# Forgetting attention, then a spectral mix: head pairs become the outer loop, mode weights are contracted by quarters of d, the decay moves into V, and each engine issues in the order of emission

## The chip, the cores and the metric

The kernel runs on one core of a Trainium2 chip. The metric is the device time of one execution in microseconds. Times are given as the median of several runs, with the lowest and highest beside it where they matter. The profile shows one execution; its span is about 2 us shorter than the time of the same run.

The names in the profiles: PE is the engine for matrix products (PEld its loads of the stationary operand), ACT the scalar, DVE the vector and POOL the general engine. POOL and SP also issue loads and stores, each to a queue of its own; the DMA moves the bytes. The row PEclk is the share of PE's full clock that the profile records as granted. A step is one pass of the changed kernel's inner loop: two heads of one batch.

## The reference, cut to what matters

```python
# q, k, v: (8, 8, 576, 64), f: (8, 8, 576); B=8, H=8, S=576, d=64
cum    = cumsum(log(clip(f, 1e-4, 1)))
scores = q @ k.T / 8 + cum[:, :, :, None] - cum[:, :, None, :]     # causal
attn   = softmax(scores);  x = (attn @ v) as (B, S, 512)
# moe_w_r, moe_w_i: (64, 512, 512), moe_w_ch: (512, 512)
X = rfft(x, axis=1)[:, :64]                       # 64 modes
Yr = Xr @ w_r - Xi @ w_i ;  Yi = Xr @ w_i + Xi @ w_r      # per mode
u = x + irfft(Y) ;  out = u + relu(u @ w_ch)
```

The mode weights are 134 MB in fp32 (2 x 64 x 512 x 512 x 4 bytes). They are read once and cast to bf16 on the way. Each is used for 8 batches only, so reading them is the largest single piece of data movement.

## The kernel before

It has three stages. Attention takes one batch after another, and a batch is four head pairs. The mode stage starts when all batches are transformed, because the contraction of a mode runs over all 512 columns of d. The output stage follows.

```python
# attention of one head pair: 64-row operands, one exponential per head and block
for hp in range(2):
    bp = hp * 64
    pscore = psA.tile([128, 512], F32, tag="sc", name="pscore")
    nc.tensor.matmul(pscore[:Mj, 0:n],
        lhsT=KTs[bp : bp + 64, s0 : s0 + Mj],
        rhs=QTs[bp : bp + 64, s0 + c0 : s0 + c0 + n], start=True, stop=True)
    pss.append(pscore)
for hp in range(2):
    nc.scalar.activation(et[:Mj, c0 : c0 + n], pss[hp][:Mj, 0:n], ACT.Exp,
        bias=biasAll[:Mj, jb, bh : bh + 1], scale=scale)      # decay as a bias
# ... (mask, AV, normalisation, transform of a whole batch: cut)

# the mode stage: one mode at a time, all of d
wpool = ctx.enter_context(tc.tile_pool(name="wpool", bufs=6))
for m in range(NM):
    wb = wpool.tile([128, 2, NEB, D], BF16, tag="wb", name="wb")
    nc.gpsimd.dma_start(wb[:, 0, :, :], moe_w_r[m].rearrange("(dc p) e -> p dc e", p=128))
    nc.gpsimd.dma_start(wb[:, 1, :, :], moe_w_i[m].rearrange("(dc p) e -> p dc e", p=128))
    A = psM.tile([128, 2, NEB, 2 * B], F32, tag="A", name="A")
    for t in range(2):
        for ebx in range(NEB):
            for dc in range(NEB):                 # contraction over the four quarters of d
                nc.tensor.matmul(A[:, t, ebx, :],
                    lhsT=wb[:, t, dc, ebx * 128 : (ebx + 1) * 128],
                    rhs=_strided(XT[:, dc, 0, m, 0:1], [[1, 2], [NM * 2, B]]),
                    start=(dc == 0), stop=(dc == NEB - 1))
    # ... (As <- A on ACT, two combining ops on DVE into YT: cut)
    if m % 8 == 3 and (m // 8) < B:
        xw_for_batch(m // 8)                      # XW = x @ w_ch of one batch
# ... (the output stage: cut)
```

The softmax here doesn't subtract the row's maximum and nothing guards it: scores larger than these inputs give would overflow.

Of the kernel before, what the change touches and what calls it, by code (L numbers as in the profile page):

```python
# [21 lines left out]
def kernel(  # L24
# [17 lines left out]
    NSB = 5  # L42
    SBLK = [128, 128, 128, 128, 64]
    NEB = D // 128
    BH = B * H
    scale = 1.0 / math.sqrt(Dh)

    const = ctx.enter_context(tc.tile_pool(name="const", bufs=1))
    xpool = ctx.enter_context(tc.tile_pool(name="xpool", bufs=1))
    wpool = ctx.enter_context(tc.tile_pool(name="wpool", bufs=6))  # L50

    x_all = xpool.tile([128, B, NSB, D], BF16, name="x_all")
    XT = xpool.tile([128, NEB, B, NM, 2], BF16, name="XT")
# [4 lines left out]
    masks.make_identity(nc, ident_bf[:])  # L58
    masks.make_identity(nc, ident_f[:])
    masks.make_upper_triangular(nc, trimask[:], val=1.0, diag=True)  # L60

    iota_p_i = const.tile([128, 1], I32, name="iota_p_i")
    nc.gpsimd.iota(iota_p_i[:], pattern=[[0, 1]], base=0, channel_multiplier=1)
    s_i = const.tile([128, NSB], I32, name="s_i")
    nc.gpsimd.iota(s_i[:], pattern=[[128, NSB]], base=0, channel_multiplier=1)
    s_f = const.tile([128, NSB], F32, name="s_f")
    nc.vector.tensor_copy(s_f[:], s_i[:])
    nc.vector.tensor_scalar(s_f[:], s_f[:], float(S - 1), None, ALU.min)
    ones_row = const.tile([1, 128], F32, name="ones_row")
    nc.vector.memset(ones_row[:], 1.0)  # L70
    negpi = const.tile([128, 1], F32, name="negpi")
    nc.vector.memset(negpi[:], -math.pi)

    bas = const.tile([128, NSB, NM, 2], BF16, name="bas")
    BI = const.tile([128, S], BF16, name="BI")
    cumT = const.tile([128, NSB, BH], F32, name="cumT")
    biasAll = const.tile([128, NSB, BH], F32, name="biasAll")
    wch = const.tile([128, NEB, D], BF16, name="wch")

    TWO_PI_OVER_S = 2.0 * math.pi / S  # L80

    with ExitStack() as sctx:
        ps_setup = sctx.enter_context(
            tc.tile_pool(name="ps_setup", bufs=2, space=bass.MemoryType.PSUM)
        )
        ssb = sctx.enter_context(tc.tile_pool(name="setup_sb", bufs=1))

        gem = ssb.tile([128, NSB], F32, name="gem")
        nc.vector.tensor_scalar(gem[:], s_f[:], 432.0, None, ALU.is_ge)
        spl = ssb.tile([128, NSB], F32, name="spl")  # L90
        nc.vector.tensor_scalar(spl[:], s_f[:], 144.0, None, ALU.add)
        sz = ssb.tile([128, NSB], F32, name="sz")
        nc.vector.scalar_tensor_tensor(
            sz[:], gem[:], -float(S), spl[:], ALU.mult, ALU.add
        )
        S0 = ssb.tile([128, NSB], F32, name="S0")
        C0 = ssb.tile([128, NSB], F32, name="C0")
        nc.scalar.activation(
            S0[:], s_f[:], ACT.Sin, bias=negpi[:, :], scale=TWO_PI_OVER_S
        )  # L100
        nc.scalar.activation(
            C0[:], sz[:], ACT.Sin, bias=negpi[:, :], scale=TWO_PI_OVER_S
        )
        Zt = ssb.tile([128, NSB, NM, 2], F32, name="Zt")
        nc.vector.memset(Zt[:, :, 0, 0], 1.0)
        nc.vector.memset(Zt[:, :, 0, 1], 0.0)
        nc.vector.tensor_scalar(Zt[:, :, 1, 0], C0[:], -1.0, None, ALU.mult)
        nc.vector.tensor_copy(Zt[:, :, 1, 1], S0[:])
        wrot = ssb.tile([128, NSB, 2], F32, name="wrot")
        nc.vector.tensor_copy(wrot[:, :, :], Zt[:, :, 1, :])  # L110
        ta = ssb.tile([128, NSB, 32], F32, name="ta")
        tb = ssb.tile([128, NSB, 32], F32, name="tb")
        M = 2
        while M < NM:
            wr = wrot[:, :, 0]
            wi = wrot[:, :, 1]
            t0 = ssb.tile([128, NSB], F32, name="t0")
            t1 = ssb.tile([128, NSB], F32, name="t1")
            nc.vector.tensor_tensor(t0[:], wr, wr, ALU.mult)
            nc.vector.tensor_tensor(t1[:], wi, wi, ALU.mult)  # L120
            t2 = ssb.tile([128, NSB], F32, name="t2")
            nc.vector.tensor_tensor(t2[:], wr, wi, ALU.mult)
            nc.vector.tensor_tensor(wrot[:, :, 0], t0[:], t1[:], ALU.subtract)
            nc.vector.tensor_scalar(wrot[:, :, 1], t2[:], 2.0, None, ALU.mult)
            Are = Zt[:, :, 0:M, 0]
            Aim = Zt[:, :, 0:M, 1]
            wr_b = _strided(wrot[:, :, 0:1], [[2, NSB], [0, M]])
            wi_b = _strided(wrot[:, :, 1:2], [[2, NSB], [0, M]])
            nc.vector.tensor_tensor(ta[:, :, 0:M], Are, wr_b, ALU.mult)
            nc.vector.tensor_tensor(tb[:, :, 0:M], Aim, wi_b, ALU.mult)  # L130
            nc.vector.tensor_tensor(Zt[:, :, M : 2 * M, 0], ta[:, :, 0:M], tb[:, :, 0:M], ALU.subtract)
            nc.vector.tensor_tensor(ta[:, :, 0:M], Are, wi_b, ALU.mult)
            nc.vector.tensor_tensor(tb[:, :, 0:M], Aim, wr_b, ALU.mult)
            nc.vector.tensor_tensor(Zt[:, :, M : 2 * M, 1], ta[:, :, 0:M], tb[:, :, 0:M], ALU.add)
            M *= 2
        nc.vector.tensor_copy(bas[:, :, :, :], Zt[:, :, :, :])
        coef = ssb.tile([128, 1], F32, name="coef")
        nc.vector.memset(coef[:], 2.0 / S)
        nc.vector.memset(coef[0:2, :], 1.0 / S)
        for sc in range(NSB):  # L140
            ns = SBLK[sc]
            bip = ps_setup.tile([128, 128], F32, tag="sps", name="bip")
            nc.tensor.transpose(
                bip[:, :ns],
                Zt[:ns, sc, :, :].rearrange("p m ri -> p (m ri)"),
                ident_f[:ns, :ns],
            )
            nc.vector.tensor_scalar(  # L148
                BI[:, sc * 128 : sc * 128 + ns], bip[:, :ns], coef[:], None, ALU.mult
            )  # L150

        ft = ssb.tile([BH, S], F32, name="ft")
        nc.sync.dma_start(ft[:], f.rearrange("b h s -> (b h) s"))
        lf = ssb.tile([BH, S], F32, name="lf")
        nc.scalar.activation(lf[:], ft[:], ACT.Ln)
        onesS = ssb.tile([BH, S], F32, name="onesS")
        nc.vector.memset(onesS[:], 1.0)
        cum = ssb.tile([BH, S], F32, name="cum")
        nc.vector.tensor_tensor_scan(
            cum[:], onesS[:], lf[:], 0.0, ALU.mult, ALU.add  # L160
        )
        cum_ps = ps_setup.tile([128, NSB, BH], F32, tag="sps2", name="cum_ps")
        for sc in range(NSB):
            ns = SBLK[sc]
            nc.tensor.transpose(
                cum_ps[:ns, sc, :],
                cum[:, sc * 128 : sc * 128 + ns],
                ident_f[:BH, :BH],
            )
        nc.vector.tensor_copy(cumT[:, 0:4, :], cum_ps[:, 0:4, :])  # L170
        nc.vector.tensor_copy(cumT[:64, 4, :], cum_ps[:64, 4, :])
        nc.vector.memset(cumT[64:128, 4, :], 0.0)
        R_ps = ps_setup.tile([128, BH], F32, tag="sps2", name="R_ps")
        nc.tensor.matmul(
            R_ps[:],
            lhsT=ones_row[0:1, :],
            rhs=cumT[0:1, 2, :],
            start=True,
            stop=True,
        )  # L180
        Rb = ssb.tile([128, BH], F32, name="Rb")
        nc.vector.tensor_copy(Rb[:], R_ps[:])
        nc.vector.tensor_tensor(
            biasAll[:, :, :],
            _strided(Rb[:, :], [[0, NSB], [1, BH]]),
            cumT[:, :, :],
            ALU.subtract,
        )

        wch_f = ssb.tile([128, NEB, D], F32, name="wch_f")  # L190
        nc.sync.dma_start(
            wch_f[:], moe_w_ch.rearrange("(eb p) e -> p eb e", p=128)
        )
        nc.vector.tensor_copy(wch[:], wch_f[:])

    with ExitStack() as actx:
        qkbf = actx.enter_context(tc.tile_pool(name="qkbf", bufs=2))
        vapool = actx.enter_context(tc.tile_pool(name="vapool", bufs=2))
        qtkt = actx.enter_context(tc.tile_pool(name="qtkt", bufs=2))
        epool = actx.enter_context(tc.tile_pool(name="epool", bufs=14))  # L200
        psA = actx.enter_context(
            tc.tile_pool(name="psA", bufs=4, space=bass.MemoryType.PSUM)
        )
        psB = actx.enter_context(
            tc.tile_pool(name="psB", bufs=2, space=bass.MemoryType.PSUM)
        )
# [366 lines left out]
```

## Time and profile before

| | before |
|---|---|
| time, median of 4 runs | 671.9 us (670.98 to 673.73) |
| attention | up to about 308 us |
| mode stage | about 308 to 613 us |
| output stage | to 671.5 us |
| weight loads | 128 of 512 KB (as bf16) |

The page of the kernel before divides the span into 40 slices of 16.8 us. A digit is the busy share in tenths; the GB/s are bytes written into the core's memory, so fp32 weights that are cast count half.

```profile
PE   0169999999999999999888895222222222225996
PEclk9999999999995555555799877555555555555998
DMA  9999391919191914003999999999999999994375
GB/s 199 185 148 150 36 120 9 98 9 99 8 100 11 97 10 26 1 1 58 202 207 206 207 206 206 206 206 206 206 206 206 206 206 207 206 206 81 134 247 184
```

The two rows PE and DMA are complements: attention fills the PE and leaves the DMA mostly idle; the mode stage fills the DMA at 206 GB/s and leaves the PE at two tenths. The table of stretches says the same in microseconds. Its columns are the busy time of each engine with the count of instructions, then the granted clock, the DMA's share (summed packet times, so it can be above 1) and GB/s.

```profile
140.00:180.00 40.00, 39.33 (x261) 19.84 (x260) 17.50 (x83) 24.55 (x57) 12.57 (x15) 1.00 0.73 45
220.00:260.00 40.00, 39.33 (x258) 19.66 (x257) 17.87 (x85) 24.23 (x58) 11.29 (x14) 0.50 0.80 50
460.00:520.00 60.00, 15.45 (x375) 12.87 (x371) 5.31 (x24) 3.19 (x12) 17.55 (x24) 0.50 1.24 206
```

The first two of these lines also show a trap. The clock row says 1.00 in one and 0.50 in the other, but the PE does the same number of matmuls (261 and 258). The timeline, with the start, duration, engine, line and operation, tells which to believe: first attention, then the output stage.

```profile
96.23 2.43 PE L351 MATMUL px<-x_all,bas 128*128 128x512 bf16 x5
...
650.70 0.38 PE L514 MATMUL pu<-y_sb,BI 128*128 128x512 bf16 x1
650.91 0.38 PE L522 MATMUL pz<-XW,ident_bf 128*128 128x512 bf16 x1
```

Inside the first group the trace has 512-column products 426 ns apart; in the output stage they are 216 ns apart. Attention runs at half rate although the row says 1.00 there. A duration is not a spacing: here 0.38 us goes with a spacing of 0.216.

Each mode takes two loads, and each waits in the queue behind others. In the list of issues the last column is the median time from issue to landing:

```profile
wb<-in_moe_w_r_dram POOLq DMA_DIRECT2D x64, 512.0 KB, 19.8
wb<-in_moe_w_i_dram POOLq DMA_DIRECT2D x64, 512.0 KB, 20.1
```

At 206 GB/s a load of 512 KB takes 2.54 us, so 20 us are about eight loads in flight.

### The profile page before, as it was taken

The numbers are of one execution on the slowest core, as the hardware profiler recorded it, in microseconds if no ns is written. First come the engines' busy times: TensorE is split into PE (matmuls) and PEld (weight loads), VectorE is DVE, ScalarE is ACT, GpSimd is POOL, SyncE is SP. The second block draws the span as 40 slices with busy tenths as digits, with TensorE's granted clock in tenths as the row PEclk, the third lists the DMA queues.
The fourth block names the chain that finished last, engine by engine and source line by source line (L and its number), as shares of the span: only waits on it lengthen the run. The fifth ranks groups of instructions, "written<-read, shape, count | busy, mean of one in ns | idle before, by whom it ended". The sixth has DMA issues, their size and how long they took to land.

```text
span 671.5 us, 10980 instructions
## 1 busy us (share of the span) xinstructions
PE 457.6 (68%) x4340; PEld 249.0 (37%) x4340; DVE 210.5 (31%) x859; ACT 236.6 (35%) x542; POOL 198.0 (29%) x260
## 2 busy tenths in 40 slices
PE   0169999999999999999888895222222222225996
PEld 0034445454545454545544453222221212123432
DVE  6224444444444444454212120000000010011574
ACT  2046656565656565671232322000000000001553
POOL 5685251515152520003322223232323323210000
PEclk9999999999995555555799877555555555555998
DMA  9999391919191914003999999999999999994375
GB/s 199 185 148 150 36 120 9 98 9 99 8 100 11 97 10 26 1 1 58 202 207 206 207 206 206 206 206 206 206 206 206 206 206 207 206 206 81 134 247 184
DMA packets 186004, 92.62 MB, mean 138 GB/s; under 512 B 115232, under 2 KB 180768, under 8 KB 185952
## 3 DMA queue, kind: packets, MB, share of 16 engines
q0 software_dynamic: 180096, 81.28, 94.6%
q1 hardware_dynamic: 5856, 10.64, 4.6%
q8 instruction: 34, 0.56, 0.3%
q14 instruction: 18, 0.15, 0.1%
HBM read 163.73 MB, written 9.44 MB: 258 GB/s over the span
## 4 chain that ended last, share of the span: by engine, by line
PE 45%; DMA 44%; DVE 5%; issue 3%; POOL 2%; ACT 0%; SPq 0%; POOLq 0%; DVEq 0%; ACTq 0%
DMA wb<-in_moe_w_r_dram 38%; PE pav L328 14%; PE pscore L293 11%; PE QTp L249 3%; PE KTp L256 3%; DMA wb<-in_moe_w_i_dram 3%; PE px L351 3%; PE pu L507 1%; PE pyw L480 1%; PE pz L529 1%; PE pu L514 1%; PE pz L522 1%; DVE x_all L337 1%; DMA qb<-in_q_dram 1%; PE pxw L435 1%
## 5 line engine op out<-in xcount | busy, mean ns | idle before, releaser
L456 PE MATMUL A<-XT,wb 128*128 128x16 bf16 x2048 | 80.6, 192 | 164.0 <-DMA wb<-in_moe_w_i_dram 85.2
L456 PEld LDWEIGHTS <-wb 128*128 128x128 bf16 x2048 | 69.3, 105 | 185.3 <-DMA wb<-in_moe_w_i_dram 94.1
L293 PE MATMUL pscore<-QTs,KTs 64*128 64x320 bf16 (+5 forms) x384 | 119.7, 404 | 0.2
L446 POOL DMA_DIRECT2D wb<-in_moe_w_r_dram x64 | 48.8, 763 | 171.6 <-DMA wb<-in_moe_w_r_dram 95.0
L464 ACT COPY As<-A 128x128 f32<-128x128 f32 x64 | 17.0, 266 | 232.5 <-PE A L456 231.1
L467 DVE TENSOR_TENSOR YT<-As 128x32 bf16<-128x32 f32 x64 | 19.6, 307 | 238.4 <-ACT As L464 238.4
L449 POOL DMA_DIRECT2D wb<-in_moe_w_i_dram x64 | 48.0, 750 | 83.3 <-DMA wb<-in_moe_w_i_dram 83.3
L228 POOL DMA_DIRECT2D vaug<-in_v_dram x40 | 34.0, 868 | 124.7 <-PE pav L328 105.3
L336 DVE RECIPROCAL rcp<-pav 128x4 f32<-128x4 f32 (+1 forms) x80 | 14.6, 183 | 107.2 <-PE pav L328 100.8
L435 PE MATMUL pxw<-wch,xT 128*128 128x512 bf16 (+1 forms) x160 | 47.9, 432 | 0.0
L293 PEld LDWEIGHTS <-KTs 64*128 64x128 bf16 (+1 forms) x384 | 31.1, 107 | 28.2 <-issue 9.9
L220 POOL DMA_DIRECT2D qb<-in_q_dram x40 | 36.2, 905 | 13.2 <-DVE BI L148 12.7
L249 PE MATMUL QTp<-ident_bf,qb 128*128 128x128 bf16 (+1 forms) x160 | 27.7, 288 | 14.8 <-issue 7.9
L224 POOL DMA_DIRECT2D kb<-in_k_dram x40 | 36.3, 908 | 2.0 <-DMA vaug<-in_v_dram 1.0
L442 ACT CAST XW<-pxw 128x512 bf16<-128x512 f32 (+1 forms) x40 | 23.3, 585 | 38.4 <-PE pxw L435 38.1
L337 DVE TENSOR_TENSOR x_all<-pav,rcp 128x256 bf16<-128x256 f32 (+1 forms) x80 | 33.6, 421 | 1.1
L539 DVE SCALAR_TENSOR_TENSOR o_sb<-pz,u_sb 128x512 f32<-128x512 f32 (+1 forms) x40 | 27.3, 689 | 13.9 <-DMA out_dram<-o_sb 5.1
L256 PE MATMUL KTp<-ident_bf,kb 128*128 128x128 bf16 (+1 forms) x160 | 28.6, 289 | 2.1 <-DMA kb<-in_k_dram 2.1
L537 ACT CAST u_sb<-pu 128x512 bf16<-128x512 f32 (+1 forms) x40 | 23.4, 584 | 15.3 <-PE pu L514 12.6
L249 PEld LDWEIGHTS <-qb 128*128 128x128 bf16 (+1 forms) x160 | 14.3, 121 | 29.0 <-issue 19.0
L470 DVE TENSOR_TENSOR YT<-As 128x32 bf16<-128x32 f32 x64 | 22.1, 345 | 0.0
L430 DVE COPY xT<-ptr 128x576 bf16<-128x576 bf16 x32 | 14.6, 462 | 23.4 <-PE ptr L425 23.4
(1386 smaller groups left out, 874.7 us busy)
## 6 DMA issues: line engine op xcount, KB each, us to landing
wb<-in_moe_w_r_dram POOLq DMA_DIRECT2D x64, 512.0 KB, 19.8
wb<-in_moe_w_i_dram POOLq DMA_DIRECT2D x64, 512.0 KB, 20.1
out_dram<-o_sb SPq DMA_DIRECT2D x32, 256.0 KB, 2.0
qb<-in_q_dram POOLq DMA_DIRECT2D x32, 128.0 KB, 4.7
kb<-in_k_dram POOLq DMA_DIRECT2D x32, 128.0 KB, 4.6
vaug<-in_v_dram POOLq DMA_DIRECT2D x32, 128.0 KB, 4.7
wch_f<-in_moe_w_ch_dram SPq DMA_DIRECT2D x1, 1024.0 KB, 5.4
out_dram<-o_sb SPq DMA_DIRECT2D x8, 128.0 KB, 2.3
```

The lines of the kernel that those rows point to most:

```text
L220: nc.gpsimd.dma_start(qb[:ns, sc, :, :], q[b, :, sc * 128 : sc * 128 + ns, :].rearrange("h p d -> p h d"),)
L224: nc.gpsimd.dma_start(kb[:ns, sc, :, :], k[b, :, sc * 128 : sc * 128 + ns, :].rearrange("h p d -> p h d"),)
L228: nc.gpsimd.dma_start(vaug[:ns, :, sc, 0:Dh], v[b, :, sc * 128 : sc * 128 + ns, :].rearrange("h p d -> p h d"),)
L249: nc.tensor.transpose(QTp[:, sc * 128 : sc * 128 + ns], qb[:ns, sc, 2 * g : 2 * g + 2, :].rearrange("p h d -> p (h d)"), ident_bf[:ns, :ns],)
L256: nc.tensor.transpose(KTp[:, sc * 128 : sc * 128 + ns], kb[:ns, sc, 2 * g : 2 * g + 2, :].rearrange("p h d -> p (h d)"), ident_bf[:ns, :ns],)
L293: nc.tensor.matmul(pscore[:Mj, 0:n], lhsT=KTs[bp : bp + 64, s0 : s0 + Mj], rhs=QTs[bp : bp + 64, s0 + c0 : s0 + c0 + n], start=True, stop= ...
L328: nc.tensor.matmul(pav[:Ms, hq, :], lhsT=et[:Mj, ccol : ccol + Ms], rhs=vaug[:Mj, h, jb, :], start=(jb == 0), stop=(jb == sb),)
L337: nc.vector.tensor_tensor(x_b[:Ms, sb, hh * 256 : hh * 256 + 256].rearrange("p (h d) -> p h d", h=4), pav[:Ms, :, 0:Dh], _strided(rcp[:Ms, ...
L435: nc.tensor.matmul(pxw[:Ms, :], lhsT=xT[:, eb, sb * 128 : sb * 128 + Ms], rhs=wch[:, eb, :], start=(eb == 0), stop=(eb == NEB - 1),)
L446: nc.gpsimd.dma_start(wb[:, 0, :, :], moe_w_r[m].rearrange("(dc p) e -> p dc e", p=128))
L449: nc.gpsimd.dma_start(wb[:, 1, :, :], moe_w_i[m].rearrange("(dc p) e -> p dc e", p=128))
L456: nc.tensor.matmul(A[:, t, ebx, :], lhsT=wb[:, t, dc, ebx * 128 : (ebx + 1) * 128], rhs=_strided(XT[:, dc, 0, m, 0:1], [[1, 2], [NM * 2, B]]),
```

## The change

Its intent is to let the weights stream while attention runs. The outer loop now goes over quarters of d (two heads each), the inner over batches: 32 steps. After 8 steps the first quarter of the transformed x is complete for all batches, and the modes' contraction over that quarter can begin. Groups of four modes by one quarter are loaded (64 groups of 2 MB as read) into a ring of 11 buffers; from step 9 on, two groups are consumed per step, and partial sums are kept in SBUF (`Yacc`). The last 16 groups (the last quarter) run after attention, with XW. Keys are padded with zeros to 128 rows per head, the exponentials of both heads and several blocks are merged, and the decay multiplies V, so that it is no bias any more. A manual schedule makes each engine issue in the order of emission. `wch` is no longer loaded at the start on SP's queue, but where the last stage begins, on POOL's queue, into memory that attention has given up.

```diff
+    NRING = 11
+    ctx.enter_context(tc.manual_schedule())
+    def emit_w_load(n):
+        dc, g = divmod(n, NG)                    # quarter of d, group of 4 modes
+        wb = wpool.tile([128, 2, MG, D], BF16, tag="wb", name="wb")
+        ...                                      # two loads on POOL, 512 KB each
+    def emit_modes(n):
+        A = psM.tile([128, NDC, MG, 2 * B], F32, tag="A", name="A")     # one buffer
+        ...                                      # 32 matmuls
+        if dc == 0:          nc.vector.tensor_copy(ysl, A[:, :, :, :])
+        elif dc < NDC - 1:   nc.vector.tensor_tensor(ysl, A[:, :, :, :], ysl, ALU.add)
+        else:                                    # last quarter: strided into YT
+            nc.vector.tensor_tensor(_strided(late["YT"][:, 0, 0, g * MG, 0:1],
+                [[B * NM * 2, NDC], [1, n8], [NM * 2, B]]), A..., ysl..., ALU.add)
+        lhsT=KTz[s % NK][h][:, jb * 128 : (jb + 1) * 128],    # zero-padded, 128 rows
+            nc.scalar.activation(E[:, :, piece * 512 : piece * 512 + w],
+                ps[:, :, 0:w], ACT.Exp, scale=scale)           # both heads, no bias
+        next_w()
+        emit_transposes(0)
+        for s in range(NS + 1):
+            if s + STG - 1 < NS:  emit_loads(s + STG - 1)
+            if s < B:             next_w()
+            ...                   # transposes(s+1), scores(s), AV(s-1), transform(s-1)
+            if s == 0:            emit_basis()
+            if s == B:
+                while nload < NRING:  next_w()
+            if s > B:
+                for j in range(2):
+                    emit_modes(2 * (s - B - 1) + j);  next_w()
+    # after attention's pools are closed:
+        wch = bsb.tile([128, NDC, D], BF16, name="wch")
+        nc.gpsimd.dma_start(wch[:], moe_w_ch.rearrange("(eb p) e -> p eb e", p=128))
+        while nmode < NDC * NG:
+            for _ in range(2):  emit_modes(nmode);  nmode += 1
+            if nx < B:  emit_xw(nx);  nx += 1
+            next_w();  next_w()
+        ...                       # output stage, cut
```

## The prediction

> **What bounds the kernel now: two stages in turn, each leaving the other's engine idle.** The 40 slices show it. Up to about 310 us the PE is 98-99% busy (39.3 of 40 us in 140-180 us) while the DMA share is 0.7 and 45 GB/s. From 340 to 600 us the DMA holds 206 GB/s flat and the PE is at most a quarter busy from 460 us on; the chain gives 38% to the real mode weights alone. The last weights land at 613 us; 58 us of output follow. The six weight buffers prefetch only about the first modes.
>
> In attention the array runs at half rate, whatever the clock row says: a 512-column product starts 430 ns after the last (five in 2.43 us), against 216 ns in the output stage (650 us). The Trainium skill, "TensorE: Matmul & The Clock Gate", Part 1, gives the same two spacings for cold and warm. Each switch between 64-row and 128-row operands costs about 110 ns more (448 columns: 480 ns instead of 373); "TensorEngine Tiling (Array Packing)", Key Properties, says that a mode switch drains the array, and the trace agrees.
>
> **What the change does.** With d-quarters outermost, modes of a quarter can run once 8 of 32 attention steps are done. Two groups (4 MB read) are consumed per step from step 9, so weights stream during attention. Zero padding removes the mode switches; decay in V merges 12 exponentials per pair into 4. It adds a partial-sum add on DVE per group and two K copies on ACT per step.
>
> **Costs, estimates from the trace.**
> - Weights: 128 DMAs at 2.54 us (512 KB at 206 GB/s) = 326 us, unchanged.
> - q and k: 73,700 packets of 128 B; saturated stretches (28-42 us, 154 GB/s) give 13 ns a packet per engine, 61 us. v, now fp32 on SP: guess 38 us.
> - Output writes at 228 GB/s: 41 us.
> - DMA floor about 470 us.
> - Steady step: DMA 4 x 2.54 + 3 = 13 us. Engines: PE at half rate 7.1k columns = 5.9 us plus 64 mode products at 42 ns = 2.7; ACT about 5 us (exponential: 0.15 us + 0.85 ns per column); DVE about 5 us. With the single pav and A buffers, in-order waits bring a step to about 11 us, so the DMA stays just ahead as the limit.
>
> **Path.** Start: POOL issues 18 small loads (0.7 us each) before the identities, then the decay chain; step 0 also holds the basis chain (about 12 us of DVE): 38 us. Eight steps of 8 us without modes: 102 us; DMA idles about 20 us here. Steps 9-29 at 13 us (DMA), the last three at 10: about 400 us. Then 16 groups with 8 batches of XW, about 9 us each: 472 us. Output 50 us: PE, DMA near 44 us. Sum **522 us, range 488 to 562**. Faster 97%, same 2%, slower 1%.
>
> **What would show it.** DMA over 90% busy near 200 GB/s from about 100 to 400 us; PE waiting for weights or q/k DMAs each step; no stretch longer than 20 us without DMA before the output; steps of about 13 us; ACT's exponentials 128, each about 1.0-1.1 us; 512-column products in the final XW/output stage at 216 ns; the final stage (after the last attention step) about 120 us.
>
> **What would make it wrong.** Steps bound by the in-order chain of exp, mask, AV, normalise, transform through single buffers: 14-16 us instead of 13 adds up to 70 us. Small v packets costing more beside the weights. The PE staying at half rate in the last XW/output stage: 40 to 60 us more. A warm PE through attention, or cheap v packets, would bring 490.

## More of the kernel before

`wch`, the bf16 copy of w_ch, is made in the setup, in the first microseconds: SP's queue loads it in fp32 (1.4 to 6.8 us in the trace), and DVE casts it.

## The result, and the profile after

The changed kernel took 564.56 us (563.41 to 565.83, 4 runs), against 671.9 us before. The ratio is 0.840, with a 95% interval of 0.837 to 0.842. Ratios here are the mean time of one kernel's fast runs over that of the other's fast runs of the same rounds, so they are not quite the ratio of the medians.

This is faster by 16%, but 42.6 us over the 522 us predicted and 2.6 us above the upper end of the range. The page of the changed kernel, in slices of 14.1 us:

```profile
PE   0417765775555555555545555647611878889996
PEclk9997789766665777666666666677555898879999
DMA  9799999999999999999999999999999790002554
GB/s 152 105 187 189 197 188 194 193 173 199 186 193 190 195 198 194 201 189 194 194 185 196 199 195 193 190 197 206 207 206 206 115 198 8 1 1 84 207 209 175
```

The DMA is now full from slice 2 on (counted from 0) to slice 32, but for slice 31. Two places are new: around slices 29 and 30 the PE has a hole (the digits 1 1), and in slices 33 to 35 the DMA is empty. The stretches:

```profile
120.00:160.00 40.00, 21.98 (x362) 16.59 (x360) 15.80 (x40) 14.91 (x21) 18.85 (x27) 0.63 1.37 190
200.00:240.00 40.00, 20.97 (x349) 16.12 (x350) 14.31 (x38) 15.02 (x21) 21.43 (x30) 0.70 1.38 198
400.00:420.00 20.00, 6.39 (x150) 5.91 (x150) 5.97 (x10) 0.46 (x1) 5.92 (x8) 0.50 1.24 206
420.00:440.00 20.00, 5.82 (x17) 2.23 (x18) 0.00 (x0) 1.76 (x3) 0.00 (x0) 0.53 1.05 174
480.00:500.00 20.00, 17.23 (x209) 11.51 (x208) 8.18 (x12) 5.65 (x11) 0.00 (x0) 0.83 0.00 1
```

Between 420 and 440 us the PE issues 17 matmuls. The PE's timeline around it shows where it stands still; the brackets give the idle time before a group and what ended it:

```profile
403.63 1.00 PE L98 MATMUL A<-XT_4038,wb 128*128 128x16 bf16 x32 [0.51 <-DVE Yacc L109]
406.02 1.00 PE L98 MATMUL A<-XT_4038,wb 128*128 128x16 bf16 x32 [1.39 <-DVE YT L112]
406.87 2.29 PE L507 MATMUL ptr<-ident_bf,x_all 128*128 128x128 bf16 x20
434.18 6.66 PE L516 MATMUL pxw<-wch,xT 128*128 128x512 bf16 x20 [25.02 <-issue]
440.68 0.95 PE L98 MATMUL A<-XT_4038,wb 128*128 128x16 bf16 x32
```

The wait is called "issue", which means that the profile has found no releaser. What the product at 434.18 reads is `xT`, which DVE had finished by 409.9, and `wch`. POOL's timeline and the list of issues tell the rest:

```profile
411.45 0.74 POOL L79 DMA_DIRECT2D wb<-in_moe_w_i_dram  x1 [1.55 <-DMA wb<-in_moe_w_i_dram]
414.45 0.74 POOL L499 DMA_DIRECT2D wch<-in_moe_w_ch_dram  x1 [2.26 <-DMA wb<-in_moe_w_r_dram]
416.81 0.74 POOL L79 DMA_DIRECT2D wb<-in_moe_w_r_dram  x1 [1.62 <-DMA wb<-in_moe_w_i_dram]
```

```profile
wch<-in_moe_w_ch_dram POOLq DMA_DIRECT2D x1, 512.0 KB, 19.6
```

POOL reaches the load of `wch` at 414.45, after weight loads each of which had to wait for an earlier one to finish. It lands 19.6 us later, at 434.1, behind the same queue of about eight loads. The PE starts at 434.18. As the PE issues in the order of emission, it could not run the mode groups behind this product: the weights of the next four (50 to 53) had landed by 406.1, and those of five more landed up to 431.5.

Inside the attention loop all went nearly as expected. In the timeline of a step, after a wait for keys:

```profile
217.51 0.71 PE L349 MATMUL tp<-ident_bf,stk_124 128*128 128x128 bf16 x5 [4.82 <-DMA stk_124<-in_k_dram]
218.55 0.63 PE L377 MATMUL ps<-QTs,KTz_0_125 128*128 128x512 bf16 x1
218.98 0.63 PE L377 MATMUL ps<-QTs,KTz_1_126 128*128 128x512 bf16 x1
```

The milestones, taken from the starts of the transform's products (predicted, then measured): the transform of step 8 at 102 and 99.9 us; a steady step 13 and 13.8 us; the first group of the last stage at 400 and 403.6; the first output product at 472 and 510.6; the end of the profiled span at 522 and 562.2.

### The profile page after: what moved, and what is told of

It is laid out like the page before. It is cut to its first block, busy times and chain, and to the rows that moved or that the text cites. A ratio compares the mean times of both kernels' runs of the same rounds, so it can differ in the third digit from the quotient of the medians.

```text
span 562.2 us, 10785 instructions
## 1 busy us (share of the span) xinstructions
PE 331.8 (59%) x4428; PEld 226.9 (40%) x4428; DVE 236.1 (42%) x600; ACT 216.6 (39%) x320; POOL 235.5 (42%) x338
## 4 chain that ended last, share of the span: by engine, by line
DMA 41%; PE 26%; issue 10%; DVE 9%; POOL 7%; ACT 6%; ACTq 0%; POOLq 0%; DVEq 0%
DMA wb<-in_moe_w_i_dram 40%; PE pxw L516 7%; PE A L98 4%; POOL wb L79 3%; PE ps L377 2%; ACT E_129 L384 2%; ACT E_130 L384 2%; DVE YT L112 2%; PE pu L571 2%; PE ptr L507 2%; DMA stk_124<-in_k_dram 2%; PE pz L575 1%; PE pz L579 1%; PE pav L411 1%; PE pu L567 1%
## 5 line engine op out<-in xcount | busy, mean ns | idle before, releaser
L98 PEld LDWEIGHTS <-wb 128*128 128x128 bf16 x2048 | 59.1, 99 | 28.0 <-issue 22.8
L516 PE MATMUL pxw<-wch,xT 128*128 128x512 bf16 x160 | 41.7, 411 | 26.8 <-issue 25.0
L523 ACT CAST XW<-pxw 128x512 bf16<-128x512 f32 x40 | 23.4, 586 | 85.9 <-PE pxw L516 85.9
L384 ACT ACTIVATE E_130<-ps 128x1024 bf16<-128x1024 f32 x64 | 50.5, 837 | 8.8 <-PE ps L377 8.3
L384 ACT ACTIVATE E_129<-ps 128x1024 bf16<-128x1024 f32 x64 | 50.3, 837 | 6.5 <-PE ps L377 5.9
L112 DVE TENSOR_TENSOR YT<-A,Yacc 128x256 bf16<-128x256 f32 x16 | 20.7, 1296 | 70.2 <-PE A L98 70.2
L435 PE MATMUL px<-bas,x_all 128*128 128x128 bf16 x160 | 20.8, 231 | 36.4 <-DVE x_all L420 36.4
L362 ACT COPY KTz_0_125<-tp 64x640 bf16<-64x640 bf16 x16 | 11.7, 730 | 74.5 <-PE tp L349 74.5
L399 DVE TENSOR_TENSOR E_130<-E_130,trimask 128x256 bf16<-128x256 bf16 (+1 forms) x64 | 19.6, 306 | 41.3 <-ACT E_130 L384 41.2
L399 DVE TENSOR_TENSOR E_129<-E_129,trimask 128x256 bf16<-128x256 bf16 (+1 forms) x64 | 19.5, 306 | 40.6 <-ACT E_129 L384 40.5
L516 PEld LDWEIGHTS <-xT 128*128 128x128 bf16 x160 | 16.1, 103 | 49.7 <-issue 28.6
L362 ACT COPY KTz_0_127<-tp 64x640 bf16<-64x640 bf16 x16 | 11.7, 732 | 62.9 <-PE tp L349 62.9
L585 DVE SCALAR_TENSOR_TENSOR uo<-pz,uo 128x512 f32<-128x512 f32 (+1 forms) x40 | 27.6, 690 | 14.1 <-ACT uo L584 14.1
L420 DVE TENSOR_TENSOR x_all<-pav,rcp 128x384 bf16<-128x384 f32 x64 | 31.4, 491 | 2.2
L377 PE MATMUL ps<-QTs,KTz_0_125 128*128 128x512 bf16 (+2 forms) x96 | 30.7, 382 | 1.6 <-ACT E_129 L384 1.5
L411 PEld LDWEIGHTS <-E_129 128*128 128x128 bf16 x480 | 24.6, 117 | 16.7 <-DVE x_all L420 8.4
L377 PE MATMUL ps<-QTs,KTz_0_127 128*128 128x512 bf16 (+2 forms) x96 | 30.1, 376 | 1.6 <-ACT E_130 L384 1.5
L411 PEld LDWEIGHTS <-E_130 128*128 128x128 bf16 x480 | 24.4, 117 | 15.3 <-DVE x_all L420 7.8
L377 PE MATMUL ps<-QTs,KTz_1_126 128*128 128x512 bf16 (+2 forms) x96 | 30.3, 378 | 0.0
```

Of the source, the lines that this page charges most:

```text
L98: nc.tensor.matmul(A[:, eb, mi, :], lhsT=wb[:, t, mi, eb * 128 : (eb + 1) * 128], rhs=XT3[:, m, c0 : c0 + 2 * B], start=(t == 0), stop=(t ...
L112: nc.vector.tensor_tensor(_strided(late["YT"][:, 0, 0, g * MG, 0:1], [[B * NM * 2, NDC], [1, n8], [NM * 2, B]],), A[:, :, :, :].rearrange( ...
L362: nc.scalar.copy(dst[hs, :], tp[hs, :])
L377: nc.tensor.matmul(ps[:, h, o : o + n], lhsT=KTz[s % NK][h][:, jb * 128 : (jb + 1) * 128], rhs=QT[s][:, jb * 128 + c0 : jb * 128 + c0 + n] ...
L384: nc.scalar.activation(E[:, :, piece * 512 : piece * 512 + w], ps[:, :, 0:w], ACT.Exp, scale=scale,)
L399: nc.vector.tensor_tensor(dg, dg, tr, ALU.mult)
```

## The experiments

All twelve kernels gave a correct result by the comparison with the reference, even `e4_half_w`, which is wrong: y is a small part of the output, and the comparison's tolerance did not see it.

The theory was: the last stage lost 24 us to `wch` landing late behind POOL's queue, and the rest of the miss is the pace of that stage. The rivals were the hand-over of memory between the stages, and steps bound by the engines rather than the DMA.

### e1_wch_early: load wch in step 8, into a tile of its own

```diff
+    wch = const.tile([128, NDC, D], BF16, name="wch")
             if s == B:
+                nc.gpsimd.dma_start(wch[:], moe_w_ch.rearrange("(eb p) e -> p eb e", p=128))
                 while nload < NRING:
-        wch = bsb.tile([128, NDC, D], BF16, name="wch")
-        nc.gpsimd.dma_start(wch[:], moe_w_ch.rearrange("(eb p) e -> p eb e", p=128))
```

> One edit to the changed kernel: the channel weights wch get a tile of their own and are loaded in step 8, not at the end. Theory (the 24.3 us in which the PE stands still before the first XW product, 409.9 to 434.2 us, is the wait for the wch load, issued last on POOL behind a full DMA queue): that gap falls below 2 us, the rest shifts, total 540 us (536 to 545). Rival (the gap is the hand-over of PSUM and SBUF from attention to the last stage, or a PE matter): gap stays over 20 us, total 560 or more. Second rival (time is given back: weights are then what the last stage waits for): gap gone but total over 550.

Measured: 541.79 us (540.31 to 543.07), ratio to before 0.805 (0.803 to 0.808). That is 22.8 us less than the changed kernel. The timeline of the PE:

```profile
410.00 2.29 PE L509 MATMUL ptr<-ident_bf,x_all 128*128 128x128 bf16 x20
412.51 5.30 PE L518 MATMUL pxw<-wch,xT 128*128 128x512 bf16 x19 [0.22 <-issue]
```

The gap is 0.22 us. The time was not given back. The theory holds; the edit changes both when `wch` is loaded and into which memory, so the next run separates these.

### e2_wch_sp: leave wch late, but take it off POOL's queue

```diff
-        nc.gpsimd.dma_start(wch[:], moe_w_ch.rearrange("(eb p) e -> p eb e", p=128))
+        wch_f = wpool.tile([128, NDC, D], F32, tag="wb", name="wch_f")
+        nc.sync.dma_start(wch_f[:], moe_w_ch.rearrange("(eb p) e -> p eb e", p=128))
+        nc.vector.tensor_copy(wch[:], wch_f[:])
```

> wch stays at its place in the program (after attention's memory is given up), but is loaded in fp32 on SP's own queue into a ring slot and cast on DVE. Theory (it was POOL's order and the 20 us of weight loads queued ahead of it, not the memory hand-over): gap of the PE at most 8 us, total 541 to 550. Rival (memory hand-over): gap stays about 20 us or more, total about 560.

Measured: 550.75 us (549.82 to 551.44), ratio 0.819. The gap was 12.7 us, larger than the 8 expected, and the total just outside the expected 541 to 550.

```profile
404.51 1.00 PE L98 MATMUL A<-XT,wb 128*128 128x16 bf16 x32 [0.52 <-DVE Yacc L109]
418.26 1.00 PE L98 MATMUL A<-XT,wb 128*128 128x16 bf16 x32 [12.75 <-DVE YT L112]
```

SP issued the load at 405.5 and it landed 9.8 us later, against 414.45 and 19.6 on POOL. About half of the stall thus went with POOL's order and queue. The other half is the load's own time beside a full stream of weights; the same fp32 load took 5.4 us in the setup of the kernel before. The split is rough, as this load writes 1 MB where POOL's writes 512 KB. The wait also has a new form: DVE, which works in order too, stood still at the cast, and so the PE waited for DVE's next add.

### e5_no_manual: let the scheduler order

```diff
-    ctx.enter_context(tc.manual_schedule())
```

> The changed kernel without the manual schedule: the scheduler may reorder. The build shows that wch keeps its place on POOL, but some 290 matmuls of the mode groups now precede the first XW product on the PE. Theory: wch still lands at about the same time, but the PE works on mode groups meanwhile, so most of the 24 us is filled: 540 us (530 to 555). Rival (emission order is what makes attention fast, or the gap isn't wch): 560 or slower.

Measured: 540.79 us (540.01 to 542.7), ratio 0.806. The PE's timeline now has the mode groups in the time in which it stood still before:

```profile
408.33 1.00 PE L97 MATMUL A<-XT,wb 128*128 128x16 bf16 x31 [1.92 <-DMA wb<-in_moe_w_i_dram]
410.83 0.20 PE L97 MATMUL A<-XT,wb 128*128 128x16 bf16 x1 [1.50 <-DMA wb<-in_moe_w_r_dram]
413.38 0.99 PE L97 MATMUL A<-XT,wb 128*128 128x16 bf16 x31 [2.35 <-DMA wb<-in_moe_w_i_dram]
```

The first XW product started at 436.3 us, so `wch` came no earlier; the PE had other work. This fits the two conditions of the loss: a late load, and an order of emission that puts its first reader ahead of work that was ready. It is not a clean test, as the scheduler reorders the whole kernel: attention's last transform also started 8 us earlier than in the changed kernel. The manual schedule as such gained nothing here: without it the changed kernel is 24 us faster, and within 1 us of `e1_wch_early` (no run has both an early `wch` and no manual schedule).

### e4_half_w: half of the weights in the loop

```diff
         for t, src in enumerate((moe_w_r, moe_w_i)):
+            if t == 1 and 16 <= n < 48:
+                continue
-                        lhsT=wb[:, t, mi, eb * 128 : (eb + 1) * 128],
+                        lhsT=wb[:, 0 if 16 <= n < 48 else t, mi, eb * 128 : (eb + 1) * 128],
```

> Wrong result on purpose: for mode groups 16 to 47 only the real weights are loaded and used twice; engine work is the same, the DMA work of a step falls from about 13.9 to 8.8 us. Theory (the steps of 13.9 us are DMA-bound and the in-order chain of the engines needs about 10 to 11 us): steps 17 to 30 take 10 to 11 us each, total 510 to 530. Rival (the in-order chain through single buffers sets 13.9 us): steps stay near 13.5 us, total 555 or more.

Measured: 485.41 us (481.64 to 486.92), ratio 0.722. The steps fell from 13.8 to 9.0 us, further than expected, and the wait for keys nearly vanished:

```profile
205.05 0.44 PE L351 MATMUL tp<-ident_bf,stk 128*128 128x128 bf16 x5 [0.28 <-DMA stk<-in_k_dram]
```

The steps of 13.8 us are therefore bound by the DMA, and the chain of the engines needs at most 9.0 us, not the 11 of the prediction. (The edit also takes two of POOL's issues out of a step, 0.74 us each; that the bytes are the limit rests on the DMA row too, full at 190 to 198 GB/s in the changed kernel. It still moves 187 GB/s here between 165 and 320 us, so even 9.0 us may be the DMA's.) The stall on `wch` was still there (21.1 us in the trace), as it should be.

### f1_yt: the last add in the order of its input

On top of `e1_wch_early`, and so are the next three.

```diff
-                _strided(late["YT"][:, 0, 0, g * MG, 0:1], [[B * NM * 2, NDC], [1, n8], [NM * 2, B]]),
-                A[...].rearrange("p e m (r b) -> p e (m r) b", r=2), ysl.rearrange(...), ALU.add,
+                late["YT"][:, :, g * MG : (g + 1) * MG, :], A[:, :, :, :], ysl, ALU.add
-        YT = bsb.tile([128, NDC, B, NM, 2], BF16, name="YT")
+        YT = bsb.tile([128, NDC, NM, 2 * B], BF16, name="YT")
-                    lhsT=YT[:, eb, b, :, :].rearrange("p m ri -> p (m ri)"),
+                    lhsT=_strided(YT[:, eb, 0, b : b + 1], [[B, 2 * NM]]),     # twice
```

> On top of e1_wch_early (541.8 us): the last add of each mode group writes YT in the order of its PSUM input instead of a strided transposed order; the readers take strides instead. Theory (in the last stage each pair of mode groups waits 1.39 us for the 1.3 us strided add, as A has one buffer): the add falls to about 0.42 us, the wait to about 0.5, 8 iterations save about 1 us each: 534 us (531 to 537). Rival (the strided weight loads of YT cost the same back, or the last stage is bound by the weight DMAs): 540 or more.

Measured: 527.62 us (525.78 to 528.53), ratio 0.784 (0.782 to 0.786): 14.2 us less than `e1_wch_early` (another chip; by the ratios 2.2% of the kernel before, 14.5 us). The groups of instructions, of the changed kernel and of this one, have line, shapes, count, busy time and mean ns:

```profile
L112 DVE TENSOR_TENSOR YT<-A,Yacc 128x256 bf16<-128x256 f32 x16 | 20.7, 1296 | 70.2 <-PE A L98 70.2
```

```profile
L112 DVE TENSOR_TENSOR YT<-A,Yacc 128x256 bf16<-128x256 f32 x16 | 6.8, 424 | 42.9 <-PE A L99 42.9
```

The strided write made a DVE operation of 256 columns three times as long. The wait of the second group fell from 1.39 to 0.52 us, as expected, but an iteration (two mode groups and one XW) fell by more, from about 10.3 to 8.2 us, and the total lies below the expected range. In this kernel the 20 transposes of x take 1.28 us in all iterations but the first, where `e1_wch_early` has 1.74 to 2.29, and the granted clock from 440 to 480 us was 1.00 instead of 0.83. It fits that the shorter waits let the PE keep its full rate; no run isolates it.

### f2_vcast: v on POOL as bf16

```diff
-        Vst = [stv.tile([128, NSB, 2, Dh + 1], F32, name=f"Vst{i}") for i in range(NV)]
+        Vst = [stv.tile([128, NSB, 2, Dh + 1], BF16, name=f"Vst{i}") for i in range(NV)]
-                (Vst[s % NV], v, nc.sync),
+                (Vst[s % NV], v, nc.gpsimd),
```

> On top of e1_wch_early (541.8 us): v loaded by POOL with a cast to bf16 (128 B written per packet) instead of fp32 on SP. The DMA-bound step of 13.9 us is 10.2 of weights and 3.7 of q, k and v, where q and k should be 1.9 by the packet cost of the kernel before (13 ns), so v's fp32 packets cost 25 ns each per engine. Theory: as bf16 on POOL they cost 13 ns, the step falls by 0.9 us to about 13.0, less about 5 us for nine more POOL issues at the start: 527 us (521 to 535). Rival (packet cost is set by the 256 B read or the steps are limited by POOL's issue): step within 0.3 us of 13.9 or longer, total 540 or more.

Measured: 592.58 us (590.94 to 594.4), ratio 0.882: about 50 us slower than `e1_wch_early`, a clear miss. Steps took 15.6 us. Three stretches within one step:

```profile
194.00:197.00 3.00, 0.00 (x0) 0.00 (x0) 0.00 (x0) 0.00 (x0) 1.32 (x2) 0.50 1.84 122
197.00:200.00 3.00, 1.89 (x13) 1.36 (x14) 0.47 (x1) 1.08 (x2) 2.76 (x5) 0.50 0.82 55
200.00:203.00 3.00, 2.99 (x40) 2.07 (x39) 1.83 (x6) 2.52 (x4) 3.00 (x6) 0.65 1.15 185
```

For about 3 us in this step the DMA carries little (55 GB/s), while POOL is busy issuing (2.76 of 3 us). This recurs in every step: of the 160 us from 170 on, 25 lie below 80 GB/s; in `e1_wch_early` none does. POOL's timeline just before shows it waiting, with small loads in hand:

```profile
193.94 0.77 POOL L164 DMA_DIRECT2D Vst<-in_v_dram  x1 [2.17 <-DMA wb<-in_moe_w_r_dram]
196.38 0.74 POOL L164 DMA_DIRECT2D Vst<-in_v_dram  x1 [1.68 <-DMA wb<-in_moe_w_i_dram]
```

Counted from issues and landings, POOL has up to eight loads in flight in each of the fourteen traces and never more, whatever their size. Nine of its thirteen loads per step are now small and stand in a row (six of ten in `e1_wch_early`). At 196.4 us all eight in flight are small; they have landed by 199.4, and POOL needs about 0.75 us to issue each of the weight loads that follow. So the eight places and POOL's single order, rather than bytes or packets, explain the dips. This is read from the trace, and no run isolates it; that this load of v on SP's queue is far better is shown. Fewer bytes on the wrong queue cost 9%.

### f3_start: weights between the first loads

```diff
-        for s in range(STG - 1):
-            emit_loads(s)
-        masks.make_identity(nc, ident_bf[:]) ...
+        emit_loads(0)
+        masks.make_identity(nc, ident_bf[:]) ...
+        next_w(); emit_loads(1); next_w(); emit_loads(2)
```

> On top of e1_wch_early (541.8 us): POOL issues only the first step's loads before the identities and the mask, and the first two weight groups are issued between the loads of steps 1 and 2. Theory (the PE waits 15.2 us for the identities behind 18 POOL issues, and the DMA loses about 10 us in the first 40 us, which the DMA-bound stage can't give back): total 534 us (530 to 537). Rival (absorbed later): 540 or more.

Measured: 540.47 us (539.84 to 541.39), ratio 0.803: no gain beyond noise over `e1_wch_early` (0.805, intervals overlap). The rival was right. The DMA moved more in the first 20 us (168 GB/s instead of 111), less in the next 20 (154 instead of 178) and between 80 and 120 us (174 instead of 188); the last transform came at 403.0 instead of 403.6 us.

### f4_rows64: 64-row keys again

```diff
-                        lhsT=KTz[s % NK][h][:, jb * 128 : (jb + 1) * 128],
-                        rhs=QT[s][:, jb * 128 + c0 : jb * 128 + c0 + n],
+                        lhsT=KTz[s % NK][0][h * 64 : h * 64 + 64, jb * 128 : (jb + 1) * 128],
+                        rhs=QT[s][h * 64 : h * 64 + 64, jb * 128 + c0 : jb * 128 + c0 + n],
```

> On top of e1_wch_early (541.8 us): the scores take 64-row operands again, as in the kernel before, instead of zero-padded 128-row keys; one key tile of 128 rows, the same two copies. Theory (array mode switches are back in every step, about 1 us of PE time, but the step waits for DMA): within 1% of 541.8. Rival (the padding is what made attention fast): 12 us or more slower.

Measured: 540.55 us (538.78 to 542.04), ratio 0.803: the same. In steps 2 to 8, which run no modes, a step took 7.4 us on average instead of 7.3. The zero padding, which the prediction counted as a part of the gain, is off the critical path in this kernel. What it is worth where the DMA is not the limit stays open: steps that wait for no load took 7.36 us here and 6.72 in `e1_wch_early`, but here at half the PE's rate (five transposes in 0.69 us, there in 0.44).

The trace also shows what the padding gives up. With 64 rows the products of the two heads start together:

```profile
79.22 0.61 PE L377 MATMUL ps<-QTs,KTz 64*128 64x512 bf16 x2
```

The second starts 3 ns after the first, and the next product 539 ns later, so the pair takes 0.54 us, mode switch included. Two padded products of 512 columns, at the same half rate, take 2 x 0.426 us. So this run does not give the price of the mode switch alone: it brings back the switches and this overlap.

### h1_no_overlap: undo the overlap alone

On top of `e1_wch_early`.

```diff
-            if s > B:
-                for j in range(2):
-                    emit_modes(2 * (s - B - 1) + j)
-                    next_w()
-        nmode = 2 * (NS - B)
+        nmode = 0
-    NRING = 11
+    NRING = 10          # room for four transforms (xtpool bufs 2 -> 4)
```

> On top of e1_wch_early (541.8 us): no mode group runs inside the attention loop; all 64 run after it, the first 8 pairs with XW beside them; the ring has 10 buffers instead of 11, to make room for four transforms. It undoes the overlap alone. Theory (overlap of the weight stream with attention is one part of the gain, a shorter attention the other): steps stay at 7 us throughout, attention ends at about 270 us, then 54 groups of 5.1 us of DMA, 52 us of output: 598 us (585 to 610), so the overlap is worth about 56 us of the 130 and the rest of the change 75. Rival (attention itself became no faster and all of the gain is overlap): 650 or more.

Measured: 614.42 us (611.22 to 616.0), ratio 0.913 (0.909 to 0.917), 4 us above the expected range. Its page, slices of 15.3 us:

```profile
PE   0436756667676656769999522222222222126996
DMA  9999999999778783009999999999999999992555
```

The smaller ring leaves one group more, 5.1 us of DMA, for the time after attention, so the edit is not quite the overlap alone. The page shows the two stages of the kernel before again, with attention ending at about 272 us instead of 308. Of the 130 us between the kernel before and `e1_wch_early`, 72.6 are thus the overlap (614.42 - 541.79), and 58 are the other changes together: a shorter attention, and a ring that holds 10 groups (16% of the weights) at its end instead of 6 of 64 modes. The expectation was 56 and 75.

### g1_basis: the setup first

On top of `f1_yt`: iota, identities and the chain that makes the transform's basis are moved ahead of the first loads, out of step 0; only the five transposes for the inverse basis stay there.

```diff
+        Zt_ = emit_basis()          # iota, identities, mask and the chain on DVE
         for s in range(STG - 1):
             emit_loads(s)
-        masks.make_identity(nc, ident_bf[:]) ...
             if s == 0:
-                emit_basis()
+                emit_bi()           # the transposes only
```

> On top of f1_yt (527.6 us): iota, identities and the transform basis come first on POOL and DVE, before the loads are issued, instead of inside step 0. Theory (f3_start gained nothing because the ring of 11 weight buffers is full before step 9 begins, so that only an earlier step 9 lets the DMA go on; the basis chain holds the PE 14.7 us in step 0): step 9 begins about 10 us earlier, total 518 us (514 to 522). Rival (the start is absorbed whatever is done): 526 or more.

Measured: 528.82 us (528.14 to 529.79), ratio 0.787 (0.785 to 0.789), against 0.784 for `f1_yt`: nothing gained. The first transform came 14 us earlier (its last product started at 35.9 instead of 49.7 us), but steps 4 to 8 then took 8.3 to 9.4 us instead of about 7, waiting for keys, and the last transform came at 405.6 instead of 405.0 us. The theory of a full ring is wrong here: the DMA was busy all along (179 to 192 GB/s from 20 to 80 us), and attention just ran into it earlier. The stream of loads, which starts at once and is full after 20 us, sets when attention ends.

### g2_all: A from the larger pool in the last stage

On top of `g1_basis`.

```diff
-        A = psM.tile([128, NDC, MG, 2 * B], F32, tag="A", name="A")
+        pool, tag = late.get("psA", (psM, "A"))      # psBig once attention is over
+        A = pool.tile([128, NDC, MG, 2 * B], F32, tag=tag, name="A")
```

> g1_basis, and in the last stage the PSUM tile of a mode group comes from the seven-buffer pool instead of its single buffer. Theory (the second group of each pair no longer waits 0.5 us for the add of the first): 8 iterations save about 0.5 us each, 3 to 6 us below g1_basis. Rival (the transposes' copies on DVE set the pace then): within 2 us of g1_basis.

Measured: 522.2 us (521.92 to 522.3), ratio 0.777 (0.775 to 0.778), 6.6 us less than `g1_basis`. Iterations of the last stage fell from 8.2 to about 7.6 us, a little more than was expected.

### g3_best: both start edits together

On top of `g2_all`, the order of `f3_start` for the first loads (`emit_loads(0); next_w(); emit_loads(1); next_w(); emit_loads(2)`).

> On top of g2_all (522.2 us): the first two weight groups are issued between the loads of steps 0, 1 and 2, as in f3_start, now that the basis no longer holds step 0. Theory (the DMA is what bounds everything up to the last stage, so time is gained only where the DMA is not full: it moves 113 GB/s in the first 20 us against 190 later, about 8 us): 516 us (513 to 519). Rival (this slack is not in reach, as with f3_start and g1_basis each alone): 521 or more. It is also the best version that these experiments point to.

Measured: 519.12 us (518.63 to 522.71), ratio 0.7735 (0.770 to 0.777), at the upper end of what was expected. The median is 3 us below `g2_all`, but the intervals overlap and the runs were on different chips, so whether this last edit gains anything is left open. The DMA moved 166 GB/s in the first 20 us, and 160 in the next. As a whole it is the fastest version here: 8% under the changed kernel, 23% under the kernel before.

## Why the prediction was right or wrong

**Right: what bounds each stage.** Before, attention and weights in turn. After, the DMA from early on, with the PE waiting 4.8 us for keys in a steady step; `e4_half_w` shows that it is the DMA and not the chain (13.8 to 9.0 us with half of the weights). Attention's end was predicted at 400 us, and the last stage's first group started at 403.6.

**Right on the sum, wrong on terms.** The step was 13.8 instead of 13 us, as q, k and v cost 3.7 us (13.83 less four loads of 2.54) instead of 3; over the 16 steps from 12 to 27 that is 15 us more. That attention's end fits all the same is luck: the three steps after the eighth took 27 us instead of 39, as their weights were loaded ahead into the ring (a reading, not tested). The first transform came 4 us later than predicted (its last product at 49.7 instead of 46 us), and the next seven steps took 7.2 instead of 8 us each. The chain of the engines was put at 11 us and needs at most 9.0. The long exponentials (96 of the 128) were as predicted, 1.02 us.

**Wrong: the step that failed.** "Then 16 groups with 8 batches of XW, about 9 us each: 472 us." The stage took 106.9 us (403.6 to 510.6) instead of 72. Of the 34.9 us in excess, 25.0 are the wait of the PE for `wch`, and 9.9 the pace: 81.9 us over 8 iterations are 10.2 us each instead of 9. `e1_wch_early` takes the stall out and lands at 541.79 us, within the predicted range; `f1_yt` and `g2_all` show two terms of the pace, the strided add of 1.3 us and the single buffer behind it. A third is PE's rate: in five of the eight iterations the 20 transposes of x took 2.29 us, in the other three 1.28. The remaining 7.7 us of the 42.6 are 3.6 in attention, 1.7 in the output stage, and the difference between span and time.

The data for the stall were in view. The kernel before showed 20 us from issue to landing on POOL's queue, and the diff showed a load with the PE's next work depending on it at the very end of that queue. The prediction used neither: its "about 9 us each" for the last stage has no term for the landing of `wch`, as if it were there. An idle PE was not in its list of what would make it wrong either. The half-rate PE that it feared in this stage came only in part: those five groups of transposes and 17 of 159 spacings of the XW products (426 ns), while 121 were 216 ns.

**Wrong: where the gain comes from.** Zero padding was listed among what is gained. The trace supports the cost of a mode switch: in the kernel before, the fifth of the five products above, with 64 rows, starts 567 ns after the fourth instead of 426. But the cost does not lie on the critical path of the changed kernel, and the padding also gives up an overlap of the two heads' products, which the prediction did not count (`f4_rows64`). Which of the other edits shortened a step without modes from 8.4 us per head pair (33.8 us per batch in the kernel before) to 7.2 is not settled.

**Wrong: no stretch without DMA over 20 us before the output.** The DMA was idle from about 464 to 513 us: the weights were all in by 465.3, and the last stage was then bound by the engines, so the lost 25 us could not be hidden behind loads.

On the skill: the prediction rested on "TensorE: Matmul & The Clock Gate", Part 1, for the two rates. The traces agree with it: 426 and 216 ns for 512 columns. The same page warns under "HAM trace caveats" that recorded clock events are unreliable; here the clock row said 1.00 at 96 us, where the spacing was 426 ns. "TensorEngine Tiling (Array Packing)", Key Properties, says that changing the tiling mode drains the array, and the 567 ns agree. "DMA: Bandwidth & Descriptors", "Issuing engines are not separate DMA queues", says that issuing from several engines "will only save the time on the sequencer". Runs are against taking this as small: on SP the w_ch load (1 MB written) landed 9.8 us after its issue and on POOL (512 KB) 19.6, behind loads in flight, and moving v from SP to POOL, with a cast, cost about 50 us.

## What to carry to other kernels

When a change makes one DMA queue busy throughout, look for every small load that stands at its end, and ask what reads it first: its latency is the queue's depth (here 20 us), and with a fixed order of emission all ready work behind that reader waits too. Cost a stage by the last of its inputs to land, not by the busy time of its engines. An edit that only lets the engines start earlier (`g1_basis`) is worth nothing while a stream of loads sets the pace; find that stream first, by halving it. Count the loads of a queue, too, and not only their bytes: here eight small ones filled POOL's queue as eight large ones did.

## What the Trainium skill lacked or had wrong

- "DMA: Bandwidth & Descriptors": the advice that spreading DMAs over issuing engines saves only usually small issue time misleads for POOL with a full queue. Moving three small loads per step for v from SP to POOL, cast included, took the kernel from 541.8 to 592.6 us; the DMA fell to 55 GB/s for 3 us of a step.
- The same page did not give, where I looked, how long a load waits on POOL's queue: here 19.6 to 20.1 us, about eight loads of 512 KB at 2.54 us. Nor does it give how many can be in flight: eight and never more in all fourteen traces, of 512 KB or of 64 KB and less.
- "TensorEngine Tiling (Array Packing)" says that a mode switch drains the array, without a number: 567 instead of 426 ns between 512-column products here, so about 140 ns.
- "TensorE: Matmul & The Clock Gate" has the two rates right (426 and 216 ns for 512 columns) and warns of the clock's records; here the record said 1.00 for stretches at half rate.
- "SBUF — State Buffer" speaks of a penalty for accesses that stride past a 16-byte line, but neither it nor the other pages that were read gives the cost for a bf16 output of DVE: 256 columns from PSUM took 1296 ns with a stride of 128 elements and 424 ns in order.
